# Cross attention and an ELU block on one core: state times w_in made per batch, one score matrix, 32x32 turns on VectorE

## The chip, the cores and the metric

The kernel runs on one core of a Trainium2 chip. The metric is the device time of one execution in microseconds (us), lower is better. In the views of the profile PE is TensorE's matmul, PEld its weight load, DVE VectorE, ACT ScalarE, POOL GpSimd and SP SyncE; L12 is line 12 of the kernel's file.

## What is computed

Eight batches of eight heads each have 512 tokens `x` and 32 rows of `state`, 64 wide. Tokens read the state and the state reads the tokens, from the same scores; both results go through a block of two matrices with ELU between them. `w_in` and `w_out` come as float64.

```python
B, H, S, Ns, D = (8, 8, 512, 32, 64)
scores = scale * np.matmul(x, state.transpose(0, 1, 3, 2))
scores = scores - scores.max(-1, keepdims=True)
a = np.exp(scores)
a /= a.sum(-1, keepdims=True) + 1e-09
xread = np.matmul(a, state)
scores2 = scale * np.matmul(state, x.transpose(0, 1, 3, 2))
...
a2 /= a2.sum(-1, keepdims=True) + 1e-09
sread = np.matmul(a2, x)
attn = np.concatenate([xread, sread], axis=2)      # (B, H, S + Ns, D)
x = attn.transpose(0, 2, 1, 3).reshape(B * (S + Ns), H * D)   # 4352 rows of 512
h = x @ w_in                                       # w_in 512 x 2048
g = np.where(h > 0.0, h, np.exp(np.minimum(h, 0.0)) - 1.0)
return g @ w_out                                   # w_out 2048 x 512
```

## The kernel before

Everything is float32; TensorE runs a float32 product as two instructions. One product of up to 512 columns fills one bank of PSUM. `ps_a` (three banks) serves attention, `ps_h` (three) the first matrix, `ps_o` (two) the second.

Setup loads the tokens of two batches and all states, turns the states (`k_bd`: 128 rows are two heads by 64, 128 columns are four heads by 32 state rows) and begins with the weights. `load_weights` fetches 512 float64 columns per partition and turns them into float32 on VectorE with seven operations; there are 16 such blocks of `w_in` and 16 of `w_out`. A block of `w_in` is 128 of the 2048 columns, all that one `ffn1` needs.

Attention of a batch is a list of 17 or 18 steps. `turn_x` turns the tokens of a pair of heads on TensorE (tile `xT`). `token_softmax` (`ts_ps`) takes tokens as rows and makes the softmax over the 32 state rows: maximum, subtraction and product on VectorE, exponential on ScalarE. `turn_token` (`tT_ps`) turns the weights back on TensorE, and `token_read` (`tr_ps`) multiplies them by the states, which gives `x2T`, the 512 model columns of what the tokens read, turned. `state_softmax` (`ss_ps`) makes the same scores once more, with state rows in the partitions, for the softmax over the tokens; its output has two halves of 64 partitions, each of one product with 64 columns of weights. `turn_state` (`sT_ps`) and `state_read` (`sr_ps`) use it.

The main loop goes over batches. `ffn1` runs 16 times for a batch: four products over the 512 model columns into `h_ps`, then ELU by a minimum on VectorE (PSUM to SBUF), an exponential on ScalarE and one last operation on VectorE. After each `ffn1` one step of the next batch's attention is emitted. Then `ffn2` runs for four groups of 128 tokens with 16 products each (`o_ps`). In batch 0 a block of `w_out` is loaded behind each `ffn1`. After the last batch, the 256 rows that the states read go through the same two matrices. A scheduler of the framework orders each engine's instructions from this program; on its engine an instruction then waits for its turn.

Of the kernel before, what the change touches and what calls it, by code (L numbers as in the profile page):

```python
# [19 lines left out]
def kernel(  # L20
# [7 lines left out]
):  # L28
    nc = tc.nc
# [17 lines left out]
    # The weights come as float64, here as the integers of the same bits.  # L47
# [5 lines left out]
    apool = ctx.enter_context(tc.tile_pool(name="attn", bufs=1))  # L53
# [3 lines left out]
    tpool = ctx.enter_context(tc.tile_pool(name="tok", bufs=2))  # L57
# [24 lines left out]
    x_t, st = {}, {}  # L82
# [9 lines left out]
    def setup():  # L92
        nc.vector.memset(v_bd, 0.0)
        make_identity(nc, ident)
        load_x(0)
# [6 lines left out]
        load_x(1)  # L102
# [15 lines left out]
        # The power of two, as the bits of a float32 with src's sign.  # L118
# [17 lines left out]
        # The mantissa, 1 to 2 times 2 ** 20: the high word's part is exact, the sum rounds.  # L136
# [18 lines left out]
    def turn_x(b, n):  # L155
        """x of a pair of heads, turned: rows (head, d), columns (r, p)."""
        ps = bank([P, R, P], "xT_ps")
        for r in range(R):
            nc.tensor.transpose(ps[:, r], x_t[b][:, r, n * P : (n + 1) * P], ident)  # L159
        nc.scalar.copy(out=st[b]["xT"][:, n], in_=ps)  # L160

    def state_softmax(b, g):
        """Rows (head of four, state row), over all tokens."""
        ps = bank([P, R, P], "ss_ps")
        for i in range(2):
# [3 lines left out]
                st[b]["xT"][:, 2 * g + i],  # L169
# [5 lines left out]
        nc.vector.reduce_max(top, ps.rearrange("p r q -> p (r q)"), axis=AX_X)  # L175
# [12 lines left out]

    def turn_state(b, g):
        ps = bank([P, R, P], "sT_ps")  # L190
        for r in range(R):
            nc.tensor.transpose(ps[:, r], st[b]["a_s"][:, g, r], ident)  # L192
        nc.scalar.copy(out=st[b]["aT_s"][:, g], in_=ps)

    def state_read(b):
        """Each pair's product of both heads with both: the two that belong are kept."""
        ps = bank([P, NP, 2 * NS], "sr_ps")
        for n in range(NP):
            i = n % 2
# [8 lines left out]
        for c in range(2):  # L208
            rows = slice(c * D, (c + 1) * D)
            nc.vector.tensor_copy(  # L210
                out=xT_state[rows, :, b * NS : (b + 1) * NS],
# [3 lines left out]
    def token_softmax(b, u):  # L215
        """Rows p, columns (r, head, state row), over the state rows; half of the r."""
        RH = R // 2
        ps = bank([P, RH, H * NS], "ts_ps")
        for i in range(RH):
            for n in range(NP):  # L220
                c = n % 2
                nc.tensor.matmul(  # L222
                    ps[:, i, n * D : (n + 1) * D],
                    st[b]["xT"][:, n, u * RH + i],
                    k_bd[:, b * G + n // 2, c * D : (c + 1) * D],
# [3 lines left out]
        top = small.tile([P, RH * H], FP32, name="top_t")  # L229
        total = small.tile([P, RH * H], FP32, name="total_t")  # L230
        a = st[b]["a_t"][:, u * RH : (u + 1) * RH].rearrange("p r (h n) -> p (r h) n", n=NS)
        s = ps.rearrange("p r (h n) -> p (r h) n", n=NS)
        nc.vector.reduce_max(top, s, axis=AX_X)
        nc.vector.tensor_tensor(out=a, in0=s, in1=bc(top, NS), op=ALU.subtract)
        nc.scalar.activation(out=a, in_=a, func=AF.Exp, scale=scale)
        nc.vector.reduce_sum(total, a, axis=AX_X)
        nc.vector.tensor_scalar(
            out=total, in0=total, scalar1=eps, scalar2=None, op0=ALU.add
        )
        nc.vector.reciprocal(out=total, in_=total)  # L240
        nc.vector.tensor_tensor(out=a, in0=a, in1=bc(total, NS), op=ALU.mult)

    def turn_token(b, g):
        ps = bank([P, R, P], "tT_ps")
        for r in range(R):
            nc.tensor.transpose(ps[:, r], st[b]["a_t"][:, r, g * P : (g + 1) * P], ident)  # L246
        nc.scalar.copy(out=st[b]["aT_t"][:, g], in_=ps)  # L247

    def token_read(b, n):
        rows = slice((n % 2) * D, (n % 2 + 1) * D)  # L250
        ps = bank([P, R, P], "tr_ps")
        nc.tensor.matmul(  # L252
            ps, v_bd[rows, b * G + n // 2], st[b]["aT_t"][rows, n // 2], start=True, stop=True
        )
        (nc.scalar.copy, nc.vector.tensor_copy)[n % 2](out=st[b]["x2T"][:, n], in_=ps)

    def begin(b):
        st[b] = dict(
            xT=apool.tile([P, NP, R, P], FP32, name="xT"),
            a_s=apool.tile([P, G, R, P], FP32, name="a_s"),  # L260
            aT_s=apool.tile([P, G, R, P], FP32, name="aT_s"),
            a_t=apool.tile([P, R, H * NS], FP32, name="a_t"),
            aT_t=apool.tile([P, G, R, P], FP32, name="aT_t"),
            x2T=tpool.tile([P, NP, R, P], FP32, name="x2T"),
        )
        turn_x(b, 0)
# [117 lines left out]
```

## Time and profile before

| | |
|---|---|
| time, median of 3 runs (lowest to highest) | 1136.9 us (1135.33 to 1138.26) |
| profiled execution: span from first to last instruction | 1135.5 us |
| TensorE busy (matmul) | 1086.1 us, 96% |
| VectorE busy | 384.5 us, 34% |
| ScalarE busy | 161.0 us, 14% |
| GpSimd busy | 18.0 us, 2% |
| HBM traffic over the span | 30 GB/s |

The page of the profile gives the span of the profiled execution and no other time of it; the span is 1.4 us below the median of the timed runs. A busy time is the union of an engine's instructions. Matmuls are pipelined, so a group's mean duration of one (593 to 599 ns for 512 columns) is longer than the distance from one to the next.

### The profile page before, as it was taken

The page shows a single profiled execution, that of the slowest core. Times are in us where ns is not written, and L with a number is a line of the kernel's source. Part 1 is how long each engine was busy: PE and PEld are TensorE (multiplying, and loading weights), DVE is VectorE, ACT ScalarE, POOL GpSimd, SP SyncE. Part 2 cuts the span into 40 slices and gives each one's busy share as a digit, 9 for nine tenths or more (in the row PEclk, how much of TensorE's full clock was granted, in tenths as well). Part 3 has the DMA queues.
Part 4 walks back from the last instruction along what each step waited for, and adds up shares of the span by engine and source line. Part 5 has one row for each costly group of instructions (what it writes and reads, how often), then busy time and mean ns, then how long its engine had stood idle before and what let it go on. Part 6 is the DMA issues. An engine that isn't in the chain of part 4 may idle for free.

```text
span 1135.5 us, 7859 instructions
## 1 busy us (share of the span) xinstructions
PE 1086.1 (96%) x3152; PEld 524.4 (46%) x3152; DVE 384.5 (34%) x742; ACT 161.0 (14%) x290; POOL 18.0 (2%) x26
## 2 busy tenths in 40 slices
PE   0679999999999999999999999999999999999998
PEld 0443454534445454534444454534444454444483
DVE  4989980441015300441015300441015300340040
ACT  0211310221012200221012200221012200110020
POOL 2000000000000000000000000000000000000000
PEclk8689999999999999999999999999999999999999
DMA  8363230000200010000200010000000000000000
GB/s 186 92 169 127 93 93 19 19 0 1 56 19 1 0 38 19 19 1 1 55 19 1 0 38 18 19 1 0 19 19 0 1 1 18 19 0 7 30 1 18
DMA packets 31588, 35.10 MB, mean 31 GB/s; under 512 B 17856, under 2 KB 26048, under 8 KB 31552
## 3 DMA queue, kind: packets, MB, share of 16 engines
q1 hardware_dynamic: 30080, 29.89, 8.6%
q0 software_dynamic: 1472, 4.72, 1.9%
q8 instruction: 24, 0.39, 0.1%
q14 instruction: 12, 0.10, 0.0%
HBM read 25.69 MB, written 8.91 MB: 30 GB/s over the span
## 4 chain that ended last, share of the span: by engine, by line
PE 94%; DVE 4%; DMA 1%; issue 0%; SPq 0%; ACT 0%
PE h_ps L286 41%; PE o_ps L305 41%; PE tr_ps L252 3%; PE sr_ps L201 3%; PE ts_ps L222 2%; PE xT_ps L159 1%; PE ss_ps L166 1%; DMA raw<-in_moe_w_in_dram 1%; DVE power L132 1%; PE sT_ps L192 1%; DVE w_in L141 1%; PE tT_ps L246 1%; DVE raw L137 0%; DVE power L128 0%; DVE power L124 0%; DVE power L119 0%
## 5 line engine op out<-in xcount | busy, mean ns | idle before, releaser
L286 PE MATMUL h_ps<-x2T,w_in 128*128 128x512 f32 x1024 | 465.3, 599 | 9.0 <-DVE g_sb L298 9.0
L305 PE MATMUL o_ps<-w_out,g_sb 128*128 128x512 f32 x1088 | 471.4, 593 | 0.0
L305 PEld LDWEIGHTS o_ps<-w_out,g_sb 128*128 128x128 f32 x1088 | 205.3, 190 | 252.3 <-issue 250.3
L286 PEld LDWEIGHTS h_ps<-x2T,w_in 128*128 128x128 f32 x1024 | 187.2, 191 | 238.1 <-issue 195.2
L295 DVE TENSOR_SCALAR e_sb<-h_ps 128x512 f32<-128x512 f32 (+1 forms) x144 | 95.1, 661 | 177.7 <-PE h_ps L286 177.5
L312 DVE COPY o_sb<-o_ps 128x512 f32<-128x512 f32 x17 | 11.8, 691 | 350.2 <-PE o_ps L305 350.2
L296 ACT ACTIVATE e_sb<-e_sb 128x512 f32<-128x512 f32 (+1 forms) x144 | 87.4, 607 | 279.6 <-DVE e_sb L295 257.9
L298 DVE SCALAR_TENSOR_TENSOR g_sb<-e_sb,h_ps 128x512 f32<-128x512 f32 (+1 forms) x144 | 93.9, 652 | 72.8 <-ACT e_sb L296 72.6
L312 ACT COPY o_sb<-o_ps 128x512 f32<-128x512 f32 x17 | 10.0, 587 | 335.4 <-PE o_ps L305 335.4
L160 ACT COPY xT<-xT_ps 128x512 f32<-128x512 f32 x32 | 18.5, 587 | 200.7 <-PE xT_ps L159 200.7
L210 DVE COPY xT_state<-sr_ps 64x128 f32<-64x128 f32 x16 | 4.6, 288 | 96.7 <-PE sr_ps L201 96.6
L252 PE MATMUL tr_ps<-aT_t,v_bd 64*128 64x512 f32 x64 | 34.8, 700 | 0.2 <-ACT aT_t L247 0.2
L106 PE MATMUL k_ps<-ident,v_bd 128*128 128x128 f32 x16 | 3.9, 426 | 31.9 <-DVE k_bd L107 18.1
L222 PEld LDWEIGHTS ts_ps<-k_bd,xT 128*128 128x128 f32 x256 | 30.7, 192 | 5.7 <-issue 5.7
L201 PEld LDWEIGHTS sr_ps<-aT_s,x_sb 128*128 128x128 f32 x256 | 30.7, 195 | 4.9 <-issue 4.3
L222 PE MATMUL ts_ps<-k_bd,xT 128*128 128x64 f32 x256 | 30.2, 272 | 0.0
L201 PE MATMUL sr_ps<-aT_s,x_sb 128*128 128x64 f32 x256 | 30.1, 276 | 0.0
L286 PE MATMUL h_ps<-xT_state,w_in 128*128 128x256 f32 x128 | 27.8, 379 | 0.0
L286 PEld LDWEIGHTS h_ps<-xT_state,w_in 128*128 128x128 f32 x128 | 24.3, 190 | 3.7 <-issue 0.5
L88 POOL DMA_DIRECT2D x_sb<-in_x_dram x16 | 14.8, 930 | 652.1 <-PE sr_ps L201 651.8
L159 PEld LDWEIGHTS xT_ps<-ident,x_sb 128*128 128x128 f32 x128 | 16.7, 148 | 14.5 <-issue 14.2
L132 DVE SCALAR_TENSOR_TENSOR power<-raw,power 128x512 uint32<-128x512 uint32 x32 | 21.8, 682 | 0.1
(45 smaller groups left out, 335.8 us busy)
## 6 DMA issues: line engine op xcount, KB each, us to landing
raw<-in_moe_w_in_dram SPq DMA_DIRECT2D x16, 512.0 KB, 3.7
raw<-in_moe_w_out_dram SPq DMA_DIRECT2D x16, 512.0 KB, 3.2
out_dram<-o_sb SPq DMA_DIRECT2D x16, 512.0 KB, 2.6
x_sb<-in_x_dram SPq DMA_DIRECT2D x16, 256.0 KB, 4.0
x_sb<-in_x_dram POOLq DMA_DIRECT2D x16, 256.0 KB, 5.5
v_bd<-in_state_dram POOLq DMA_DIRECT2D x4, 128.0 KB, 7.4
out_dram<-o_sb SPq DMA_DIRECT2D x8, 64.0 KB, 1.7
```

The lines of the kernel that those rows point to most:

```text
L132: nc.vector.scalar_tensor_tensor(out=power, in0=hi, scalar=0x80000000, in1=power, op0=ALU.bitwise_and, op1=ALU.bitwise_or,)
L159: nc.tensor.transpose(ps[:, r], x_t[b][:, r, n * P : (n + 1) * P], ident)
L160: nc.scalar.copy(out=st[b]["xT"][:, n], in_=ps)
L201: nc.tensor.matmul(ps[:, n], x_t[b][:, r, n * P : (n + 1) * P], st[b]["aT_s"][:, n // 2, r, i * D : (i + 1) * D], start=(r == 0), stop=(r ...
L222: nc.tensor.matmul(ps[:, i, n * D : (n + 1) * D], st[b]["xT"][:, n, u * RH + i], k_bd[:, b * G + n // 2, c * D : (c + 1) * D], start=True, ...
L252: nc.tensor.matmul(ps, v_bd[rows, b * G + n // 2], st[b]["aT_t"][rows, n // 2], start=True, stop=True)
L286: nc.tensor.matmul(ps, w_in[:, co, fo * P : (fo + 1) * P], xT[:, co], start=(co == 0), stop=(co == NP - 1),)
L295: nc.vector.tensor_scalar(out=e, in0=ps, scalar1=0.0, scalar2=None, op0=ALU.min)
L296: nc.scalar.activation(out=e, in_=e, func=AF.Exp)
L298: nc.vector.scalar_tensor_tensor(out=g[fo], in0=e, scalar=-1.0, in1=ps, op0=ALU.add, op1=ALU.max)
L305: nc.tensor.matmul(ps, g[fo][:, c * P : (c + 1) * P], w_out[:, fo], start=(fo == 0), stop=(fo == FO - 1),)
L312: (nc.scalar.copy, nc.vector.tensor_copy)[c % 2](out=o_sb[:, c % 2], in_=ps)
```

## The change

The tokens' weights times state times `w_in` are grouped the other way round. `make_m` multiplies the states of a batch by 512 columns of `w_in` (tile `m_sb`: 256 rows of four heads by state row twice, 512 columns), four times per batch, and `ffn1` contracts over those 256 rows: two products instead of four. `token_read` and `x2T` go. The scores are made once, with state rows in the partitions (`scores`, tile `s_ps`). For the softmax over the state rows VectorE turns the scores in blocks of 32x32 (`t_sb`), takes maximum and sum, GpSimd subtracts and multiplies, ScalarE makes the exponential; `turn_tokens` turns the blocks back on VectorE (tile `aT`). ELU's exponential now reads PSUM on ScalarE, and the minimum (with 1) follows on VectorE in SBUF. A block of `w_in` is now 512 columns of 128 rows, and the first `make_m` is emitted behind all 16 blocks. Token order within a batch, loads and `ffn2` stay.

```diff
-    apool = ctx.enter_context(tc.tile_pool(name="attn", bufs=1))
+    apool = ctx.enter_context(tc.tile_pool(name="attn", bufs=2))
+    xtpool = ctx.enter_context(tc.tile_pool(name="xT", bufs=4))
+    atpool = ctx.enter_context(tc.tile_pool(name="aT", bufs=4))
+    mpool = ctx.enter_context(tc.tile_pool(name="m", bufs=2))
...
-    def load_w_in(fo):
-        load_weights(w_in[:, :, fo * P : (fo + 1) * P], w_in_v[:, :, fo * P : (fo + 1) * P])
+    def load_w_in(c, n):
+        cols = slice(c * 512, (c + 1) * 512)
+        load_weights(w_in[:, n : n + 1, cols], w_in_v[:, n : n + 1, cols])
...
+    def scores(b, g):
+        ps = bank([P, S], "s_ps")
         for i in range(2):
             nc.tensor.matmul(
                 ps[i * D : (i + 1) * D],
                 k_bd[:, b * G + g, i * D : (i + 1) * D],
-                st[b]["xT"][:, 2 * g + i],
+                st[b, g, i],
...
+        t = apool.tile([P, NB, NS], FP32, name="t_sb")
+        nc.vector.transpose(t.rearrange("p k n -> p (k n)"), ps)
...
+        nc.vector.reduce_max(top_t, t, axis=AX_X)
+        nc.gpsimd.tensor_tensor(out=t, in0=t, in1=bc(top_t, NS), op=ALU.subtract)
+        nc.scalar.activation(out=t, in_=t, func=AF.Exp, scale=scale)
...
+        nc.vector.reduce_sum(total_t, t, axis=AX_X)
...
+        nc.gpsimd.tensor_tensor(out=t, in0=t, in1=bc(total_t, NS), op=ALU.mult)
+        st[b, g, "t"] = t
+
+    def turn_tokens(b, g):
+        st[b, g, "aT"] = atpool.tile([P, S], FP32, name="aT")
+        nc.vector.transpose(st[b, g, "aT"], st[b, g, "t"].rearrange("p k n -> p (k n)"))
...
+    def make_m(b, c):
+        m_t[b, c] = mpool.tile([P, G, 512], FP32, name="m_sb")
+        for g in range(G):
+            ps = bank([P, 512], "m_ps")
+            for i in range(2):
                 nc.tensor.matmul(
+                    ps[i * D : (i + 1) * D],
+                    k_bd[:, b * G + g, i * D : (i + 1) * D],
+                    w_in[:, 2 * g + i, c * 512 : (c + 1) * 512],
                     start=True,
                     stop=True,
                 )
+            (nc.scalar.copy, nc.vector.tensor_copy)[g % 2](out=m_t[b, c][:, g], in_=ps)
...
     def attention(b):
+        for g in range(G):
+            steps += [lambda g=g, i=i: turn_x(b, g, i) for i in range(2)]
+            steps += [lambda g=g: scores(b, g)]
+        for g in range(G):
+            steps += [lambda g=g: turn_tokens(b, g)]
+            steps += [lambda g=g: turn_state(b, g)]
+            steps += [lambda g=g: state_read(b, g)]
...
+    def elu(ps, g, fo):
+        e = epool.tile([P, n], FP32, tag="e", name="e_sb")
+        nc.scalar.activation(out=e, in_=ps, func=AF.Exp)
+        nc.vector.tensor_scalar(out=e, in0=e, scalar1=1.0, scalar2=None, op0=ALU.min)
...
+    def ffn1(g, b, fo):
+        for k in range(G):
+            nc.tensor.matmul(
+                ps,
+                m_t[b, fo // 4][:, k, fo % 4 * P : (fo % 4 + 1) * P],
+                st[b, k, "aT"],
...
+    todo = [lambda c=c, n=n: load_w_in(c, n) for c in range(FC) for n in range(NP)]
+    for f in attention(0):
         f()
+        if todo:
+            todo.pop(0)()
+    for f in todo:
+        f()
+    make_m(0, 0)
...
         for fo in range(FO):
-            ffn1(g, xT, fo)
+            ffn1(g, b, fo)
+            if fo % 4 == 1 and fo // 4 + 1 < FC:
+                make_m(b, fo // 4 + 1)
...
+            if c == 2 and b + 1 < B:
+                make_m(b + 1, 0)
```

How the instructions stand now, at three places. The first is TensorE in the ffn1 stage of a middle batch, between the last token score or state score and the turn behind it (`x4` is a count of products). Before:

```order
L166 MATMUL ss_ps<-xT,k_bd 64x512 x2
L286 MATMUL h_ps<-x2T,w_in 128x512 x4
L166 MATMUL ss_ps<-xT,k_bd 64x512 x2
L286 MATMUL h_ps<-x2T,w_in 128x512 x4
L246 MATMUL tT_ps<-ident,a_t 128x128 x4
```

After, at the same place; `s_ps` are the scores, `m_ps` the states times `w_in`:

```order
L253 MATMUL m_ps<-w_in,k_bd 64x512 x4
L175 MATMUL s_ps<-xT,k_bd 64x512 x2
L290 MATMUL h_ps<-aT,m_sb 128x512 x4
L224 MATMUL sT_ps<-ident,a_s 128x128 x4
L290 MATMUL h_ps<-aT,m_sb 128x512 x2
L233 MATMUL sr_ps<-aT_s,x_sb 128x64 x8
L290 MATMUL h_ps<-aT,m_sb 128x512 x2
L253 MATMUL m_ps<-w_in,k_bd 64x512 x4
```

An `ffn1` is two products, a make_m of four stands in one piece, and the state read follows the scores after three `ffn1` and one turn.

The second is TensorE at the end of batch 0, whose `o_ps` products need the blocks of `w_out` as they are converted. Before, then after:

```order
L305 MATMUL o_ps<-w_out,g_sb 128x512 x4
L286 MATMUL h_ps<-x2T,w_in 128x512 x4
L201 MATMUL sr_ps<-aT_s,x_sb 128x64 x8
L305 MATMUL o_ps<-w_out,g_sb 128x512
L201 MATMUL sr_ps<-aT_s,x_sb 128x64 x8
L305 MATMUL o_ps<-w_out,g_sb 128x512 x47
L286 MATMUL h_ps<-x2T,w_in 128x512 x4
```

```order
L253 MATMUL m_ps<-w_in,k_bd 64x512
L166 MATMUL xT_ps<-ident,x_sb 128x128 x4
L175 MATMUL s_ps<-xT,k_bd 64x512
L315 MATMUL o_ps<-w_out,g_sb 128x512 x2
L290 MATMUL h_ps<-aT,m_sb 128x512
L175 MATMUL s_ps<-xT,k_bd 64x512
L315 MATMUL o_ps<-w_out,g_sb 128x512 x2
L290 MATMUL h_ps<-aT,m_sb 128x512
L315 MATMUL o_ps<-w_out,g_sb 128x512 x2
L290 MATMUL h_ps<-aT,m_sb 128x512 x3
L315 MATMUL o_ps<-w_out,g_sb 128x512 x34
L290 MATMUL h_ps<-aT,m_sb 128x512 x2
```

Ahead of the 34 `o_ps` products there now stand 38 `h_ps` products (32 of batch 0, 6 of batch 1), six make_m, 40 turns of `xT` and five `s_ps` steps from the program's start; before, only batch 0's `h_ps` stand ahead of the last 47.

The third is ScalarE at the first of these places: the exponential of the states' weights (`a_s`), that of the turned scores (`t_sb` now, `a_t` before), those of ELU (`e_sb`) and the copies of the turned weights (`aT_s`). Before:

```order
L235 ACTIVATE a_t<-a_t 128x512
L296 ACTIVATE e_sb<-e_sb 128x512
L180 ACTIVATE a_s,total<-ss_ps,top 128x512
L296 ACTIVATE e_sb<-e_sb 128x512
L180 ACTIVATE a_s,total<-ss_ps,top 128x512
```

After:

```order
L260 COPY m_sb<-m_ps 128x512
L192 ACTIVATE a_s,total<-s_ps,top 128x512
L279 ACTIVATE e_sb<-h_ps 128x512
L200 ACTIVATE t_sb<-t_sb 128x512
L279 ACTIVATE e_sb<-h_ps 128x512
L226 COPY aT_s<-sT_ps 128x512
L279 ACTIVATE e_sb<-h_ps 128x512 x2
```

The exponential of the turned scores, whose input comes from GpSimd, stands one ELU exponential behind that of the states, with the next ELU exponential and the copy for the state read queued behind it.

## Rows read from the trace of the kernel before

**Rows 1.** The page: span, and busy time of the engines.

```profile
span 1135.5 us, 7859 instructions
...
PE 1086.1 (96%) x3152; PEld 524.4 (46%) x3152; DVE 384.5 (34%) x742; ACT 161.0 (14%) x290; POOL 18.0 (2%) x26
```

**Rows 2.** Windows: stretch, length, each engine's busy us, granted clock, DMA share, GB/s.

```profile
40.00:60.00 20.00, 16.89 (x77) 10.90 (x76) 15.34 (x38) 6.14 (x12) 0.00 (x0) 0.74 0.26 77
60.00:80.00 20.00, 17.04 (x85) 10.68 (x84) 18.68 (x42) 2.88 (x5) 1.87 (x2) 0.97 0.64 170
80.00:165.30 85.30, 78.56 (x216) 35.99 (x217) 85.20 (x184) 15.51 (x27) 2.21 (x2) 0.95 0.36 114
198.20:326.14 127.94, 127.94 (x370) 59.99 (x369) 33.55 (x60) 18.89 (x34) 1.76 (x2) 1.00 0.06 17
```

**Rows 3.** The chain that ended last: start us, us, what; batch 0's end, last batch, tail.

```profile
157.81 40.40 PE o_ps L305 x94
...
965.84 54.93 PE h_ps L286 x128
1020.78 54.93 PE o_ps L305 x128
1075.71 27.63 PE h_ps L286 x128
1103.34 27.48 PE o_ps L305 x64
```

**Rows 4.** The same chain within one middle batch, one row of each kind.

```profile
198.20 3.43 PE h_ps L286 x8
201.64 0.44 PE xT_ps L159 x4
...
217.13 1.73 PE ts_ps L222 x16
218.86 3.49 PE h_ps L286 x8
...
227.57 1.01 PE ss_ps L166 x4
228.58 3.63 PE h_ps L286 x8
...
244.59 1.05 PE tr_ps L252 x2
...
281.37 3.52 PE sr_ps L201 x32
```

**Rows 5.** The timeline of VectorE: first conversion, one inside a block, the last.

```profile
16.81 0.43 DVE L119 TENSOR_SCALAR power<-raw 128x512 uint32<-128x512 uint32 x1 [13.81 <-DMA raw<-in_moe_w_in_dram]
...
21.36 0.68 DVE L132 SCALAR_TENSOR_TENSOR power<-raw,power 128x512 uint32<-128x512 uint32 x1
21.96 0.42 DVE L119 TENSOR_SCALAR power<-raw 128x512 uint32<-128x512 uint32 x1
22.29 0.42 DVE L137 TENSOR_SCALAR raw<-raw 128x512 uint32<-128x512 uint32 x1
...
164.65 0.69 DVE L144 SCALAR_TENSOR_TENSOR w_out<-w_out,power 128x512 f32<-128x512 f32 x1
```

**Rows 6.** Groups by line and shape: count, busy us, mean ns, idle before.

```profile
L295 DVE TENSOR_SCALAR e_sb<-h_ps 128x512 f32<-128x512 f32 x128 | 88.4, 690 | 171.6 <-PE h_ps L286 171.4
...
L166 PE MATMUL ss_ps<-xT,k_bd 128*64 128x512 f32 x64 | 17.3, 617 | 0.5 <-DVE a_t L234 0.5
...
L234 DVE TENSOR_TENSOR a_t<-ts_ps,top_t 128x512 f32<-128x512 f32 x16 | 10.9, 685 | 0.2
```

**Rows 7.** The timeline while GpSimd issues two transfers in the front.

```profile
61.50 1.87 POOL L88 DMA_DIRECT2D x_sb<-in_x_dram  x2 [53.61 <-PE sr_ps L201]
...
62.81 0.79 DVE L137 TENSOR_SCALAR raw<-raw 128x512 uint32<-128x512 uint32 x1
```

**Rows 8.** Groups by line: the one elementwise operation of GpSimd.

```profile
masks.py:199 POOL TENSOR_SCALAR_AFFINE_SELECT ident<-ident 128x128 f32<-128x128 f32 x1 | 0.3, 306 | 0.1
```

More of the change, by code (lines that the diff above doesn't have):

```diff
@@ L38 @@
     FO = DF // P
+    FC = DF // 512
     SB = S + NS
+    NB = S // 32
     scale = 1.0 / math.sqrt(D)
@@ L101, in setup @@
             )
-        load_x(1)
+        for b in range(2):
+            load_x(b)
         for k in range(0, B * G, 4):
@@ L210, in state_read @@
             nc.vector.tensor_copy(
-                out=xT_state[rows, :, b * NS : (b + 1) * NS],
+                out=xT_state[rows, 2 * g : 2 * g + 2, b * NS : (b + 1) * NS],
                 in_=ps[rows, :, c * NS : (c + 1) * NS],
             )
[L215 to L221, printed above, removed]
+    def make_m(b, c):
+        m_t[b, c] = mpool.tile([P, G, 512], FP32, name="m_sb")
+        for g in range(G):
+            ps = bank([P, 512], "m_ps")
+            for i in range(2):
                 nc.tensor.matmul(
-                    ps[:, i, n * D : (n + 1) * D],
-                    st[b]["xT"][:, n, u * RH + i],
-                    k_bd[:, b * G + n // 2, c * D : (c + 1) * D],
+                    ps[i * D : (i + 1) * D],
+                    k_bd[:, b * G + g, i * D : (i + 1) * D],
+                    w_in[:, 2 * g + i, c * 512 : (c + 1) * 512],
                     start=True,
@@ L228, in token_softmax @@
                 )
[L229 to L266, printed above, removed]
-    def attention(b):
-        steps = [lambda: begin(b)]
-        steps += [lambda n=n: turn_x(b, n) for n in range(1, NP)]
-        steps += [lambda u=u: token_softmax(b, u) for u in range(2)]
-        steps += [lambda g=g: state_softmax(b, g) for g in range(G)]
-        steps += [lambda g=g: turn_token(b, g) for g in range(G)]
-        steps += [lambda n=n: token_read(b, n) for n in range(NP)]
-        steps += [lambda g=g: turn_state(b, g) for g in range(G)]
-        steps += [lambda: state_read(b)]
+            (nc.scalar.copy, nc.vector.tensor_copy)[g % 2](out=m_t[b, c][:, g], in_=ps)
@@ L277, in attention @@
+    def attention(b):
+        steps = []
+        for g in range(G):
[5 more added lines that the diff above has]
+            steps += [lambda g=g: state_read(b, g)]
         if b + 2 < B:
@@ L279, in attention, with ffn1_state @@
         return steps
-    def ffn1(g, xT, fo):
-        n = xT.shape[-1]
-        ps = ps_h.tile([P, n], FP32, tag="h", name="h_ps")
+    def elu(ps, g, fo):
+        n = ps.shape[-1]
+        e = epool.tile([P, n], FP32, tag="e", name="e_sb")
+        nc.scalar.activation(out=e, in_=ps, func=AF.Exp)
+        nc.vector.tensor_scalar(out=e, in0=e, scalar1=1.0, scalar2=None, op0=ALU.min)
+        g[fo] = gpool.tile([P, n], FP32, tag="g", name="g_sb")
+        nc.vector.scalar_tensor_tensor(
+            out=g[fo], in0=e, scalar=-1.0, in1=ps, op0=ALU.add, op1=ALU.max
+        )
+    def ffn1(g, b, fo):
+        ps = ps_h.tile([P, S], FP32, tag="h", name="h_ps")
+        for k in range(G):
[3 more added lines that the diff above has]
+                st[b, k, "aT"],
+                start=(k == 0),
+                stop=(k == G - 1),
+            )
+        elu(ps, g, fo)
+    def ffn1_state(g, fo):
+        ps = ps_h.tile([P, B * NS], FP32, tag="h", name="h_ps")
         for co in range(NP):
@@ L288, in ffn1 @@
                 w_in[:, co, fo * P : (fo + 1) * P],
-                xT[:, co],
+                xT_state[:, co],
                 start=(co == 0),
@@ L314 @@
     setup()
-    for i, f in enumerate(attention(0)):
-        f()
-        if i >= 4 and i % 4 == 0:
-            load_w_in(i // 4 - 1)
-    begun = i // 4
-    for fo in range(begun, FO):
-        load_w_in(fo)
+    todo = [lambda c=c, n=n: load_w_in(c, n) for c in range(FC) for n in range(NP)]
+    for f in attention(0):
+        f()
+        if todo:
[3 more added lines that the diff above has]
+    make_m(0, 0)
     for b in range(B):
@@ L345 @@
     for fo in range(FO):
-        ffn1(g, xT_state, fo)
+        ffn1_state(g, fo)
     o_sb = opool.tile([P, 2, DM], FP32, name="o_sb")
```

51 lines of the change are left out of this document (24 added, 27 removed).

## The prediction

> **What bounds the kernel now.** I read the busy shares first: TensorE is busy for 1086.1 of the 1135.5 us [rows 1]. The page gives the span alone as the profiled execution's time; the median of the timed runs is 1136.9 us, 1.4 more, and I add that 1.4 at the end. A busy share is a mean over stages, so I next read windows by stage [rows 2]: from 198.20 to 326.14 us, one middle batch, TensorE is busy all the time and VectorE for 33.55 of 127.94 us; from 80 to 165.30 us VectorE is busy for 85.20 of 85.30 us. So there are two stages, a front that VectorE fills with the conversion of the weights, and a long rest that TensorE fills. The chain of work shows the same [rows 3]: from 157.81 us on, nothing but TensorE pieces follow each other to 1130.82 us. What the change is worth is thus TensorE's saving in the rest, plus whatever happens to the moment at which the front lets go.
>
> **One middle batch on TensorE, before.** The chain inside it [rows 4] prices every step. Eight h instructions (four float32 products, two instructions each) take 3.43 us, 0.429 each. A turn of four 128x128 blocks takes 0.44. A ts step takes 1.73, and the h block behind it 3.49 instead of 3.43: 1.79 together. An ss step takes 1.01, and the h block behind it 3.63: 1.21 together. A tr step takes 1.05 plus the same 0.20: 1.25. The state read takes 3.52. There are eight turns (4 xT, 2 tT, 2 sT: 3.52), two ts (3.58), two ss (2.42), four tr (5.00), one state read (3.52), 128 h and 128 o instructions (54.93 each, as in the last batch [rows 3]): 127.90, where the rows show 326.14 - 198.20 = 127.94.
>
> **The same batch after.** ffn1 contracts over 256 columns of M instead of 512 of the model: 64 h instructions fewer, -27.47. The ts steps go (-3.58), the two tT turns (-0.88), the four tr steps (-5.00). The s steps are the old ss steps. New are four make_m per batch, of 4 products or 8 instructions each, with k_bd as 64-column weights and 512 columns streamed. No row shows it; the nearest is ss, the same shape [rows 4, 6]: four instructions of 617 ns mean fit into 1.01 us, so the two halves of the output run side by side, two by two (2 x 0.43), and 1.21 - 0.86 = 0.35 is the price of going into that form and back. make_m streams two such groups in one go: 2 x 0.86 + 0.35 = 2.07. Bounds: 1.72 if nothing is paid for the change of form, 2.42 if each group pays. I take 2.07, since both groups stand together in the order. Four: +8.28. The batch comes to 127.94 - 27.47 - 3.58 - 0.88 - 5.00 + 8.28 = 99.3. The last batch has no attention behind it and three make_m: 54.93 + 27.46 + 6.2 = 88.6. The tail (27.63 + 27.48) stays.
>
> **The front.** VectorE's first conversion starts at 16.81 us and its last ends at 165.3 [rows 5], 148.5 us, of which 6.0 idle (4.66 and 1.32 [rows 2]): 142.5 of work. The 32 conversions stay. By the order of the changed program, up to its last conversion: 16 minima of ELU now read SBUF, not PSUM; 690 ns [rows 6] against 0.42 us for the like form over SBUF [rows 5], -4.3. Operations of 0.68 follow each other at 0.60, those of 0.42 at 0.33 [rows 5]. Four copies of x2T go: -2.4. Six copies of M come ahead of that row: +3.6. Four more small xT_state copies: +1.0. One reduction of the next batch: +0.6. Eight elementwise operations (685 ns [rows 6]) go to GpSimd and eight 32x32 turns come: no row shows such a turn; between 0.42 (the fast form) and twice 685 ns this is -2 to +5, and I take 0, one element a cycle like the rest. Sum: 141.0, no relief for the front. To it come the old 6.0 idle and new waiting. GpSimd's eight elementwise operations of batches 0 and 1 lie in this stretch. Their price: one operation on 128x128 took 306 ns [rows 8], four times that is 1.22 for 128x512; bounds 0.69 (VectorE's own) and 2.45 (two inputs, one after the other); I take 1.4. When GpSimd works, VectorE's operations beside it can stretch: 0.79 us instead of 0.42 while GpSimd issued two transfers [rows 7]. If each GpSimd operation held VectorE throughout, that is 8 x 1.4 = 11 us. Besides, M of the first columns is emitted behind all w_in conversions, so the first h can start only behind 61 us of VectorE's work and some 9 of waits, at about 87 us, and TensorE has 79 us of ordered work (38 h, 30 o, six make_m and the rest) between there and the end of the front: both engines are nearly full, and a delay of one is passed on, up to 5 us. New waiting 0 to 16, taken as 8. The front ends at 16.8 + 141.0 + 6 + 8 = 172 us instead of 165.
>
> The Trainium skill ("SBUF — State Buffer", Who interferes with whom) says that GpSimd and a VectorE operation in a 2-port mode, or with two SBUF inputs, fully block each other for the whole instruction. By it the 11 us are paid in full and the front ends near 175; the stretched row agrees in kind, as an estimate only, since that GpSimd work was descriptors.
>
> **What remains behind the front.** In the order, 34 o products stand behind the last conversion (29.2 us: rows 3's 40.40 for 94 instructions, 68 here). Batch 1 has by then 6 h products, one make_m, two turns and one s step done: 99.3 - 5.15 - 2.07 - 0.88 - 1.21 = 90.0. Then five batches (496.5), the last (88.6), the tail (55.1): 759.4 us. The last copy and transfer take 1135.5 - 1130.8 = 4.7 as before.
>
> **Waits inside a batch.** ffn1 has half the work, so VectorE and ScalarE have less cover. VectorE: 16 x (0.34 + 0.60) for ELU, two score steps of 3.8, four copies and small ones, some 26 us in an ffn1 stage of 42 us; no bound. But ScalarE's queue is in order, and the exponential of the turned scores stands there ahead of the exponential of an h block and of the copy of aT_s, which the state read needs. From the end of an s step: maximum 0.60, scaling 0.08, turn 0.60, maximum 0.60, GpSimd 1.4, exponential 0.63 and about 1.0 of handovers make 4.9; then exponential 0.63 and copy 0.59: 6.1. TensorE meanwhile does three h blocks and one turn, 3 x 1.72 + 0.44 = 5.6. So 0.5 to 1 us is missing once a batch, and each us that GpSimd takes longer is one more. Bounds 0 (GpSimd 0.69) to 4 us a batch; I take 1.4: 10 us for seven batches.
>
> The Trainium skill ("GPSIMD Engine Reference", 3.1 Elementwise) measures tensor_tensor at 1.96 times VectorE's time; against 0.60 this is an estimate of 1.2 us, and the sum would be some 3 us less. No row here shows such an operation.
>
> **Sum.** 172 + 759.4 + 10 + 4.7 = 946 us of span, 947 as a time: 190 us less, 17%.
>
> **Rivals.**
> *GpSimd blocks and is blocked all the way.* If its operations take about 4 us each, because VectorE holds it off again and again, then each of the 14 groups delays both the exponential and the turn behind the second operation by 2.6 us. TensorE has one to two h blocks in hand (three PSUM buffers), so about 3 of 5.2 us come through: 14 x 3 = 42 more in place of 10, and the front 11 rather than 8: 982. For it: rows 7, and that VectorE is full in the front. Against: in a middle batch VectorE has 26 us of work in 42 us of ffn1, so GpSimd finds it idle often.
> *The two halves of make_m do not run side by side.* Then 8 x 0.43 + 0.35 = 3.79 instead of 2.07, for 26 make_m behind the front +45: 992. Against it is the ss row.
> *Slower than before.* It takes one thing: GpSimd's elementwise operation at 10 us or more. There are 28 in the loop, each in series with ScalarE's and VectorE's queues, and 190 us over 28 is 6.8 beyond the 1.4 assumed and about 2 of slack. At 12 us: 946 + 28 x (12 - 3.4) = 1187. Against it speaks 306 ns for 128x128.
> *The front hides the gain.* If VectorE stayed the bound beyond batch 0, the saving would shrink. It doesn't: behind the last conversion it has 27 us of work in 99.
>
> **How the numbers follow.** Forecast (TensorE stays the bound, waits up to 3 us a batch): 0.70, and its own range is 918 to 972. GpSimd rival: 0.18. Halves in turn: 0.05. Slower: 0.02. Better than all terms (no idle in the front, 158; make_m at 1.72; no waits): 158 + 750 + 4.7 + 1.4 = 914, and beyond: 0.05. The range 915 to 990 takes in the forecast, the front's bounds and most of the GpSimd rival. A measurement of this kernel tells about 0.3% from no change: faster 0.97, within 0.01, slower 0.02.
>
> **What will show it.** Right: middle batches of 99 to 101 us with TensorE full; make_m at about 2.07; the last w_out conversion near 172 us; GpSimd's operations between 1.2 and 2 us. Wrong: TensorE idle ahead of sr or h with ScalarE or VectorE as the releaser (GpSimd rival); make_m near 3.8; VectorE's conversions stretched beside GpSimd all through the front, or a front past 185 us; a turn on VectorE above 0.7 us.

## The result, and the profile after

The changed kernel takes 932.4 us (median of four runs, 930.75 to 932.92) where the kernel before takes 1136.6 us on the same chip (1135.33 to 1138.26): 0.820 of it, 95% interval 0.8188 to 0.8211. The forecast was 947 us, 1.6% too high. The page of the changed kernel's profile, span and busy times, against [rows 1]:

```profile
span 931.1 us, 6560 instructions
...
PE 872.7 (94%) x2512; PEld 401.3 (43%) x2512; DVE 363.1 (39%) x774; ACT 156.9 (17%) x290; POOL 53.1 (6%) x58
```

TensorE lost 213.4 us of busy time and the span 204.4 us, so nearly all of it came through. The windows by stage are cut at the same stages as [rows 2]; the first row here is the whole stretch of the weights' conversion.

```profile
16.80:165.37 148.57, 108.83 (x323) 48.47 (x323) 142.38 (x316) 26.11 (x48) 13.53 (x12) 0.87 0.41 121
...
40.00:60.00 20.00, 16.04 (x56) 10.51 (x56) 17.14 (x42) 3.70 (x7) 7.11 (x6) 0.58 0.43 105
60.00:80.00 20.00, 7.10 (x20) 1.74 (x19) 18.36 (x41) 1.76 (x3) 0.00 (x0) 0.67 0.52 160
80.00:165.37 85.37, 78.65 (x221) 32.20 (x221) 84.99 (x188) 17.72 (x32) 6.42 (x6) 0.96 0.36 111
286.58:386.16 99.58, 99.58 (x290) 44.51 (x290) 30.45 (x64) 18.42 (x34) 6.04 (x6) 1.00 0.08 22
```

The two stages are still there. From 80 us to the last conversion VectorE is busy for 84.99 of 85.37 us; in a middle batch TensorE is busy without a gap. New is the row from 60 to 80 us, in which TensorE works for 7.1 us where it worked for 17.0 before: M of the first columns has to wait for all of `w_in`. The end of the front is still 165.37 us (165.3 before); what that wait costs, the run m_early below tells. The chain of work that ended last, against [rows 3]:

```profile
165.53 2.58 PE h_ps L290 x6
168.11 29.27 PE o_ps L315 x68
...
230.01 41.20 PE o_ps L315 x96
...
329.16 41.20 PE o_ps L315 x96
...
816.43 54.93 PE o_ps L315 x128
871.37 27.63 PE h_ps L303 x128
898.99 27.48 PE o_ps L315 x64
```

A middle batch is 329.16 - 230.01 = 99.15 us (127.94 before, 99.3 forecast). The same chain inside one middle batch, against [rows 4]:

```profile
290.88 1.87 PE m_ps L253 x8
292.75 0.59 PE xT_ps L166 x4
...
302.29 1.87 PE m_ps L253 x8
304.16 0.86 PE s_ps L175 x4
305.01 3.63 PE h_ps L290 x8
308.64 0.44 PE sT_ps L224 x4
309.08 1.72 PE h_ps L290 x4
310.80 0.00 issue
310.80 2.00 PE sr_ps L233 x16
...
314.57 1.87 PE m_ps L253 x8
316.44 1.91 PE h_ps L290 x4
...
320.51 1.73 PE sr_ps L233 x16
```

A make_m is 1.87 us and lengthens what stands behind it by 0.15 (an `xT` turn, 0.59 for 0.44) or 0.19 (h, 1.91 for 1.72): 2.02 to 2.06, where 2.07 was forecast. Where a score step stands directly behind it (304.16), the form of the product does not change and 0.35 us is saved. Of waiting there is 0.27 us. It lies inside the state read, whose weight load starts only with it (310.80 us), behind the copy of `aT_s`: the first state read takes 2.00 us where the second has 1.73. Groups by line and shape (busy us, mean ns of one, idle before), against [rows 6]:

```profile
L279 ACT ACTIVATE e_sb<-h_ps 128x512 f32<-128x512 f32 x128 | 76.2, 595 | 300.4 <-PE h_ps L290 295.9 <-DVE raw L144 4.0
L253 PE MATMUL m_ps<-w_in,k_bd 128*64 128x512 f32 x256 | 68.1, 622 | 1.5 <-ACT xT L168 0.8 <-ACT m_sb L260 0.7
L280 DVE TENSOR_SCALAR e_sb<-e_sb 128x512 f32<-128x512 f32 x128 | 54.3, 424 | 82.3 <-ACT e_sb L279 82.3
...
L199 POOL TENSOR_TENSOR t_sb<-t_sb,top_t 128x512 f32<-128x512 f32 x16 | 17.8, 1115 | 570.0 <-DVE top_t L198 445.4 <-DVE total L202 122.3 <-DVE total_t L209 2.3
L213 POOL TENSOR_TENSOR t_sb<-t_sb,total_t 128x512 f32<-128x512 f32 x16 | 17.5, 1092 | 38.9 <-DVE total_t L212 38.9
L218 DVE STREAM_TRANSPOSE aT<-t_sb 128x512 f32<-128x512 f32 x16 | 11.3, 708 | 8.5 <-POOL t_sb L213 8.5
...
L206 DVE TENSOR_SCALAR a_s<-a_s,total 128x512 f32<-128x512 f32 x16 | 10.7, 666 | 0.2
```

GpSimd's operations take 1.1 us (forecast 1.4, with 1.2 to 2 named as the sign of being right), the 32x32 turn 0.71, the minimum 0.42 where it took 0.69 from PSUM.

### The profile page after: what moved, and what is told of

Its sections match the earlier page's. It is cut to its first block, busy times and chain, and to the rows that moved or that the text cites. A ratio compares the mean times of both kernels' runs of the same rounds, so it can differ in the third digit from the quotient of the medians.

```text
span 931.1 us, 6560 instructions
## 1 busy us (share of the span) xinstructions
PE 872.7 (94%) x2512; PEld 401.3 (43%) x2512; DVE 363.1 (39%) x774; ACT 156.9 (17%) x290; POOL 53.1 (6%) x58
## 4 chain that ended last, share of the span: by engine, by line
PE 88%; DVE 8%; DMA 3%; SPq 1%; ACT 0%; issue 0%; POOL 0%; DVEq 0%; ACTq 0%
PE o_ps L315 49%; PE h_ps L290 23%; PE m_ps L253 6%; PE h_ps L303 3%; DMA raw<-in_moe_w_in_dram 3%; PE sr_ps L233 3%; PE s_ps L175 2%; PE xT_ps L166 2%; DVE power L139 1%; DVE w_in L148 1%; DVE power L126 1%; DVE raw L144 1%; PE sT_ps L224 1%; DVE power L131 1%; DVE power L135 1%; DVE w_in L151 0%
## 5 line engine op out<-in xcount | busy, mean ns | idle before, releaser
L290 PE MATMUL h_ps<-aT,m_sb 128*128 128x512 f32 x512 | 242.1, 606 | 12.8 <-DVE m_sb L260 12.6
L290 PEld LDWEIGHTS h_ps<-aT,m_sb 128*128 128x128 f32 x512 | 92.3, 193 | 123.1 <-issue 82.7
L279 ACT ACTIVATE e_sb<-h_ps 128x512 f32<-128x512 f32 (+1 forms) x144 | 82.4, 572 | 335.4 <-PE h_ps L290 295.9
L280 DVE TENSOR_SCALAR e_sb<-e_sb 128x512 f32<-128x512 f32 (+1 forms) x144 | 59.0, 410 | 98.4 <-ACT e_sb L279 98.4
L253 PE MATMUL m_ps<-w_in,k_bd 128*64 128x512 f32 x256 | 68.1, 622 | 1.5 <-ACT xT L168 0.8
L260 DVE COPY m_sb<-m_ps 128x512 f32<-128x512 f32 x32 | 22.0, 688 | 91.0 <-PE m_ps L253 89.5
L199 POOL TENSOR_TENSOR t_sb<-t_sb,top_t 128x512 f32<-128x512 f32 x16 | 17.8, 1115 | 570.0 <-DVE top_t L198 445.4
L233 PEld LDWEIGHTS sr_ps<-aT_s,x_sb 128*128 128x128 f32 x256 | 33.9, 209 | 10.9 <-ACT aT_s L226 6.4
L253 PEld LDWEIGHTS m_ps<-w_in,k_bd 128*64 128x64 f32 x256 | 15.8, 138 | 46.5 <-issue 35.3
L233 PE MATMUL sr_ps<-aT_s,x_sb 128*128 128x64 f32 x256 | 34.5, 292 | 1.4 <-ACT aT_s L226 1.3
L166 PE MATMUL xT_ps<-ident,x_sb 128*128 128x128 f32 x128 | 21.4, 295 | 3.1 <-DVE xT_state L242 3.0
L260 ACT COPY m_sb<-m_ps 128x512 f32<-128x512 f32 x32 | 18.8, 586 | 22.9 <-PE m_ps L253 22.9
```

The costliest lines, as they stand in the source:

```text
L166: nc.tensor.transpose(ps[:, r], x_t[b][:, r, (2 * g + i) * P : (2 * g + i + 1) * P], ident)
L233: nc.tensor.matmul(ps[:, i], x_t[b][:, r, (2 * g + i) * P : (2 * g + i + 1) * P], st[b, g, "aT_s"][:, r, i * D : (i + 1) * D], start=(r == 0),
L253: nc.tensor.matmul(ps[i * D : (i + 1) * D], k_bd[:, b * G + g, i * D : (i + 1) * D], w_in[:, 2 * g + i, c * 512 : (c + 1) * 512], start=Tr ...
L260: (nc.scalar.copy, nc.vector.tensor_copy)[g % 2](out=m_t[b, c][:, g], in_=ps)
L279: nc.scalar.activation(out=e, in_=ps, func=AF.Exp)
L280: nc.vector.tensor_scalar(out=e, in0=e, scalar1=1.0, scalar2=None, op0=ALU.min)
```

## The experiments

Ratios are to the kernel before, with 95% intervals. "The front's end" is the end of the last conversion of `w_out`; "o" is the start of the first long row of o products in the chain (168.11 us in the changed kernel).

### GpSimd's operations doubled (pool_twice)

```diff
+        nc.gpsimd.tensor_tensor(out=t, in0=t, in1=bc(top_t, NS), op=ALU.subtract)
...
+        nc.gpsimd.tensor_tensor(out=t, in0=t, in1=bc(ones, NS), op=ALU.mult)
```

> The changed kernel with each of GpSimd's elementwise operations followed by a second one of the same size (the maximum is subtracted twice, which the softmax cancels, and the product is multiplied by one). Theory (no slack is left between the exponential of the turned scores and the state read): 1.1 us more come through once a batch, 7 to 8 us, and 2 to 4 in the front: 939 to 945 us. Rival A (GpSimd is hidden): 932 to 935 us. Rival B (GpSimd stands in series everywhere): 28 x 1.1 and the front, 963 us or more.

967.6 us, 0.852 (0.850 to 0.8535): 35 us more than the changed kernel, and my theory fell. The time lies in the range of rival B; whether each operation costs alike, as rival B has it, the next two runs tell. 7.5 us of it are in the front (o at 175.64 us) and 5.5 in each of four middle batches ((760.51 - 341.88) / 4 = 104.66 us); the batch shown here, the one ahead of them, takes 103.78 (238.10 to 341.88), 4.6 more. The timeline of this kernel in a middle batch shows the way; L201 and L202 are the two subtractions, L216 and L217 the two products, `aT` the first group's turn, `top` the second group's maximum:

```profile
312.07 1.03 PE L177 MATMUL s_ps<-xT,k_bd 128*64 128x512 f32 x4
...
313.50 1.05 POOL L217 TENSOR_TENSOR t_sb<-t_sb,ones 128x512 f32<-128x512 f32 x1
314.58 0.71 DVE L222 STREAM_TRANSPOSE aT<-t_sb 128x512 f32<-128x512 f32 x1 [1.69 <-POOL t_sb L217]
...
315.22 0.65 DVE L264 COPY m_sb<-m_ps 128x512 f32<-128x512 f32 x1
315.79 0.67 DVE L186 TENSOR_REDUCE top<-s_ps 128x1 f32<-128x512 f32 x1
...
319.12 1.05 POOL L202 TENSOR_TENSOR t_sb<-t_sb,top_t 128x512 f32<-128x512 f32 x1
...
319.16 1.29 DVE L209 TENSOR_SCALAR a_s<-a_s,total 128x512 f32<-128x512 f32 x1
320.20 0.63 ACT L203 ACTIVATE t_sb<-t_sb 128x512 f32<-128x512 f32 x1 [2.27 <-POOL t_sb L202]
320.74 0.58 ACT L283 ACTIVATE e_sb<-h_ps 128x512 f32<-128x512 f32 x1
321.21 0.58 ACT L230 COPY aT_s<-sT_ps 128x512 f32<-128x512 f32 x1
...
321.84 0.32 PE L237 MATMUL sr_ps<-aT_s,x_sb 128*128 128x64 f32 x1 [2.95 <-ACT aT_s L230]
```

The second group's scores end at 313.0 us, but VectorE stands in front of the first group's turn, which waits 1.69 us for GpSimd, and a copy is queued behind it too; the maximum starts at 315.8, 2.8 us after the scores instead of 0.9 in the changed kernel. Then the doubled subtraction holds ScalarE's queue, in which the copy of `aT_s` stands behind the exponential of the turned scores. Both together are the 2.95 us for which TensorE waits. The rest of the 4.6 us comes behind the wait: the state read takes 2.42 us instead of 1.73 and the h block behind it 3.03 instead of 1.77, at a granted clock of 0.72 between 323 and 329 us. The changed kernel has next to no slack here: its copy of `aT_s` ends 5.73 us after the scores, and TensorE has 5.79 us of other work.

### Which of the two operations (sub_twice, mul_twice)

Each doubles one of the two lines of the diff above.

> GpSimd's subtraction is doubled, its product not (a second subtraction of the same maximum, so the weights' values change; the amount of work does not). Theory: what counts is the way from the second group's scores to aT_s, which ScalarE's queue makes pass through the subtraction but not through the product. In a middle batch the doubled subtraction then adds its own 1.1 us and some 0.45 us by which the first group's turn holds VectorE when the second group's maximum is due: 1.6 us of waiting at the state read, and 0 to 2 us of slower TensorE behind it, 2 to 3.5 us a batch; with some 4 us at the front: 945 to 956 us, and each middle batch shows one wait of 1.3 to 2 us ahead of sr_ps with aT_s as the releaser. Rival (every us on GpSimd costs alike, by the shared port or by any of its two consumers): half of what both doublings cost, 949 us here and 949 us for the doubled product.

> GpSimd's product is doubled (the second time by ones), its subtraction not. Theory: the product is not on the way to aT_s; it counts only through the first group's turn, behind which the second group's maximum waits on VectorE: 0.45 us a batch at most, and up to 4 us at the front: 933 to 939 us, no wait of more than 1.2 us ahead of sr_ps in a middle batch. Rival (every us on GpSimd costs alike): 949 us.

958.8 us, 0.8434 (0.8418 to 0.845), for the subtraction; 941.2 us, 0.8281 (0.8265 to 0.8298), for the product. They cost 26.5 and 8.8 us, not the same, so the rival is out; but both lie some 2 to 3 us above the theory's ranges. The product costs 1.06 us in most middle batches (330.67 to 430.87: 100.20), one wait of 1.05 us ahead of the state read, more than twice the 0.45 that I gave: the first group's turn ends at 305.93 us, 0.5 after the scores, and two operations of ELU, the copy of `m_sb` and the maximum all stand behind it. The subtraction costs 4.1 us a batch ((752.33 - 339.28) / 4 = 103.26), more than its wait of 2.0 us. Windows of this kernel from the start of that wait on (columns as in rows 2) show the rest:

```profile
315.60:317.60 2.00, 0.00 (x0) 0.00 (x0) 1.97 (x4) 1.64 (x4) 0.32 (x1) 1.00 0.02 4
317.60:324.69 7.09, 7.09 (x22) 4.66 (x24) 3.17 (x9) 0.45 (x1) 1.05 (x1) 0.52 0.00 1
324.69:332.36 7.67, 7.67 (x38) 4.33 (x38) 3.35 (x6) 2.86 (x5) 0.00 (x0) 1.00 0.00 0
```

After 2 us in which TensorE did nothing, its granted clock is 0.52 for the next 7.09 us, close to the lower of its two levels (1.2 of 2.4 GHz), and then 1.00 again: the state read takes 3.68 instead of 1.73 us, the h block behind it 3.41 instead of 1.77, 3.6 us for a wait of 2. The five middle batches take 102.83 to 104.50 us (this one is 104.50), and what comes behind the wait is 1.9 to 3.6 us; why they differ was not tried. Behind the wait of 1.05 us of mul_twice the clock stays at 1.00 in four of the five middle batches. In the other one (531.08 to 632.92: 101.84 us) the h block behind the state read takes 3.07 us instead of 1.77 and the make_m behind that 2.21 instead of 1.87, 1.6 us for a wait of 1.05; the window of that h block:

```profile
614.92:617.99 3.07, 3.07 (x6) 0.81 (x7) 1.99 (x5) 0.00 (x0) 1.17 (x2) 0.55 0.00 0
```

### GpSimd's two operations on VectorE (vector_elem)

```diff
-        nc.gpsimd.tensor_tensor(out=t, in0=t, in1=bc(top_t, NS), op=ALU.subtract)
+        nc.vector.tensor_tensor(out=t, in0=t, in1=bc(top_t, NS), op=ALU.subtract)
```

and the product likewise.

> The changed kernel with the two elementwise operations of the turned scores on VectorE instead of GpSimd. Theory: eight of them lie in the front, 8 x 0.60 = 4.8 us, less some 1 to 2 us by which GpSimd stretched VectorE there; middle batches stay at 99 us, since VectorE has room: 932 to 937 us. Rival (the move to GpSimd is worth something in every batch): 4 x 0.6 a batch come through, 948 us or more.

931.0 us, 0.8195 (0.8183 to 0.8208): no different from the changed kernel's 932.4, 1 us below the theory's range, and the rival is out. So this part of the change is worth nothing. In a middle batch the 0.27 us of waiting is gone (o at 229.43 and 328.32: 98.89); each operation takes 0.68 us there instead of 1.05 and more, and needs no handover to another engine. In the front, eight more operations of VectorE did not make it end later: 165.09 against 165.37 us. Part of the reason is in the groups of VectorE over the conversions: beside GpSimd, the first bit operation of a conversion (L126) takes 469 ns in the mean, the last of a `w_in` block (L151) 713, and ELU's minimum 451; here 429, 682 and 418. Times their 31, 16 and 16 that is 1.2 + 0.5 + 0.5 = 2.3 us, by which VectorE is slower beside GpSimd, while GpSimd saves it eight operations at 0.60, 4.8 us. The difference, 2.5 us, and the 0.3 by which the front even ended sooner, stay open; the records of a few of VectorE's operations are missing in either trace, so its busy times over the front are not exact enough for that.

### ELU as before (elu_old)

```diff
-        nc.scalar.activation(out=e, in_=ps, func=AF.Exp)
-        nc.vector.tensor_scalar(out=e, in0=e, scalar1=1.0, scalar2=None, op0=ALU.min)
+        nc.vector.tensor_scalar(out=e, in0=ps, scalar1=0.0, scalar2=None, op0=ALU.min)
+        nc.scalar.activation(out=e, in_=e, func=AF.Exp)
```

> The changed kernel with ELU in its old order (minimum from PSUM on VectorE, then the exponential on ScalarE). Theory (VectorE sets the front, TensorE the rest): 16 minima of batch 0 cost 0.27 us more each, so the front ends 4.3 us later, the middle batches stay at 99.2 us: 936 to 937 us. Rival (the new order is what keeps ffn1 fed now that it is half as long): TensorE waits in ffn1, batches of 101 to 104 us, 945 to 965 us.

933.4 us, 0.8216 (0.8204 to 0.8228), about 1 us more than with the new ELU, with overlapping intervals: less than the theory's, and the rival is out. The relief of the front is real: it ends at 169.13 us, 3.76 later than in the changed kernel (4.3 forecast). But o starts at 169.52, only 1.4 later, for in the changed kernel TensorE still has 2.58 us of h to do when the front lets go, and here TensorE has all but 0.4 us of that behind it when the last conversion ends. In each middle batch 0.17 us come back (330.40 - 231.42 = 98.98), with a first state read of 1.82 us instead of 2.00.

### M as one chain of two products (m_serial)

```diff
                 nc.tensor.matmul(
-                    ps[i * D : (i + 1) * D],
-                    k_bd[:, b * G + g, i * D : (i + 1) * D],
+                    ps,
+                    k_bd[:, b * G + g],
                     w_in[:, 2 * g + i, c * 512 : (c + 1) * 512],
-                    start=True,
-                    stop=True,
+                    start=(i == 0),
+                    stop=(i == 1),
```

M becomes a sum of two products here, so the output is another; the instructions and their sizes along the tokens stay.

> make_m with both products 128 weight columns wide into the whole bank, the second added to the first, so that they cannot run side by side (M is then a sum of two products, not the right M). Theory: a make_m takes 8 x 0.43 = 3.43 us instead of 2.07 and pays no change of form: +1.36 for each of the 26 behind the front: 967 us, up to 8 more if the six in the front come through. Rival (the halves did not overlap before either, and make_m is cheap for another reason): 930 to 936 us.

966.9 us, 0.8503 (0.8489 to 0.8517), as expected. The chain inside a middle batch of this kernel:

```profile
305.91 3.43 PE m_ps L253 x8
309.34 1.01 PE s_ps L175 x4
...
319.64 3.43 PE m_ps L253 x8
323.07 1.72 PE h_ps L290 x4
```

Eight instructions take 3.43 us instead of 1.87, and nothing behind them is lengthened. A batch takes 335.60 - 230.84 = 104.76 us, 5.6 more. Eight instructions in 1.87 us are less than eight times 0.43, so in the changed kernel they do overlap. The pairing of the two halves is worth 34.5 us, and the rival of the forecast in which they do not run side by side is out.

### The regrouping alone (regroup_only)

The kernel before with `make_m`, two products per `ffn1` and no `token_read`; its own two score matrices, turns on TensorE and ELU stay.

```diff
-        for co in range(NP):
+        for k in range(G):
             nc.tensor.matmul(
                 ps,
-                w_in[:, co, fo * P : (fo + 1) * P],
-                xT[:, co],
+                m_t[b, fo // 4][:, k, fo % 4 * P : (fo % 4 + 1) * P],
+                st[b]["aT_t"][:, k].rearrange("p r q -> p (r q)"),
```

> The kernel before with one part of the change alone: make_m and an ffn1 of two products, w_in in blocks of 512 columns; the tokens' softmax is still made on its own scores and turned on TensorE. Theory: a middle batch is 127.94 - 27.47 - 5.00 + 8.28 = 103.8 us and the last 88.6, the front within 5 us of the changed kernel's: 958 us, 952 to 966. Rival (the single score matrix is worth as much as the regrouping): 1000 us or more.

965.5 us, 0.8493 (0.848 to 0.8505), at the upper end. A middle batch takes 344.53 - 240.89 = 103.64 us (127.94 before): the regrouping is 171 of the 204 us, and the rest of the change (one score matrix, turns on VectorE, the new ELU) the other 33. Of these, 4.5 in each of five middle batches are TensorE's ts steps and turns, 3.6 more lie between the o of batch 0 and that of batch 1 (65.48 us for 61.90), and 7.3 are the later start of o (175.41 against 168.11), for the front ends only at 174.40 us.

### The first M earlier (m_early)

```diff
     for f in attention(0):
         f()
         if todo:
             todo.pop(0)()
+        if len(todo) == 12:
+            make_m(0, 0)
     for f in todo:
         f()
-    make_m(0, 0)
```

> The changed kernel with the first make_m emitted behind the first four blocks of w_in instead of behind all sixteen. Theory: TensorE begins ffn1 some 20 us earlier, but w_out is converted no sooner, so the last conversion stays at 165 us and the time moves by at most 3 us: 929 to 935. Rival (TensorE's wait of 12.6 us for the first copy of M is lost time): 920 us or less.

931.6 us, 0.8198 (0.8185 to 0.821): the same as the changed kernel. There TensorE waits 12.6 us for its first `m_sb`. Here M is ready early, and the same h waits 10.9 us for ELU instead, which VectorE does only between conversions. The front ends at 162.07 us, 3.3 sooner, and o starts at 166.26, 1.85 sooner, too little for the medians to tell. An idle TensorE cost 1.85 us at most there, because VectorE is what sets the front's end.

### A shorter conversion (conv_short, conv_early, conv_vector)

If VectorE sets the front, fewer operations on it must shorten the whole. Three operations, shown below, make a float32 out of the bits of a float64 instead of seven. They hold for weights of a magnitude below 2 and not below 2^-126, and cut the last bits off instead of rounding. conv_early adds the edit of m_early, conv_vector that of vector_elem to both.

```diff
+        nc.vector.tensor_scalar(
+            out=power, in0=hi, scalar1=3, scalar2=0x3FFFFFF8,
+            op0=ALU.logical_shift_left, op1=ALU.bitwise_and,
+        )
+        nc.vector.scalar_tensor_tensor(
+            out=power, in0=hi, scalar=0x80000000, in1=power,
+            op0=ALU.bitwise_and, op1=ALU.bitwise_or,
+        )
+        nc.vector.scalar_tensor_tensor(
+            out=dst.bitcast(U32), in0=lo, scalar=29, in1=power,
+            op0=ALU.logical_shift_right, op1=ALU.bitwise_or,
+        )
```

> The changed kernel with three VectorE operations for a block of weights instead of seven (exponent and mantissa bits shifted together; the low bits are cut off instead of rounded, and it holds for magnitudes below 2 only). Theory: 32 x (3.15 - 1.54) = 51 us less on VectorE in the front; TensorE then has to do its 838 us from its first ffn1 at about 58 us on: 895 to 912 us. Rival (the transfer of 17 MB of weights sets the front): 920 us or more.

> Both: three operations for a block of weights, and the first make_m behind the first four blocks of w_in. Theory: with VectorE no longer the bound of the front, TensorE's start counts: its first ffn1 some 10 us earlier than with the short conversion alone, 885 to 902 us. Rival (transfers or VectorE still set the front): the same time as with the short conversion alone.

> The shorter conversion and the early make_m as in conv_early, and the two elementwise operations on VectorE instead of GpSimd. Theory: with VectorE no longer full in the front, its eight more operations there cost nothing, and the wait ahead of the state read (0.27 us a middle batch) goes as it did in vector_elem: 896 to 898.5 us. Rival (the front of conv_early still hangs on VectorE at places, and eight operations of 0.6 us more are passed on): 900 to 905 us.

903.6, 899.5 and 898.8 us, ratios 0.7949 (0.7935 to 0.7962), 0.7913 (0.7902 to 0.7925) and 0.7907 (0.7893 to 0.7921). The front now ends at 118.9 us in conv_short and 115.3 in conv_early, 46 to 50 us sooner, and 29 to 33 come through. Windows of conv_short say why not all:

```profile
60.00:80.00 20.00, 20.00 (x63) 7.47 (x63) 15.62 (x35) 7.71 (x15) 1.05 (x1) 1.00 0.56 192
80.00:117.00 37.00, 37.00 (x119) 18.16 (x118) 36.81 (x76) 8.93 (x16) 5.86 (x5) 1.00 0.55 171
```

From 60 us on TensorE is busy all the time, though VectorE still converts until 118.9: the bound has passed to TensorE 58.9 us before the conversions end, and I conclude, without a run that shows it, that a conversion saved after that would shorten nothing. An M made earlier is worth 4 us there (conv_early), where it was worth nothing while VectorE was full. The first two lie in their theories' ranges; conv_vector is 0.3 us above its own and below its rival's. conv_vector and conv_early are not told apart: the batch gains 0.27 us (295.91 - 197.02 = 98.89), and the long o row from which that is counted begins 1.4 us later (197.02 against 195.58).

## Why the prediction was right, and where its sizes were off

**Bound and saving.** The forecast that TensorE stays the bound behind the front and VectorE in it holds in every window above. The middle batch came out at 99.15 us for 99.3 without waits and 100.7 with them. Against the 99.3 the differences are small and in part cancel, which is luck: make_m 2.02 to 2.06 for 2.07, one change of form fewer (-0.35), a wait of 0.27. m_serial shows that the two halves do run side by side.

**The front.** This is the first mis-sized term: "new waiting", taken as 8 us, measured as 2.5. 172 us were forecast for its end and 165.37 measured. VectorE's work was put at 141.0 us without stretching and is 142.38 with it, about 2.3 of it by GpSimd. Idle were 6.2 us where 6 and "new waiting" of 8 were taken. So of the 8, waiting makes 0.2 and stretching 2.3 (0 to 11 was its bound). Four more products of GpSimd in the front (mul_twice) let it end only 0.45 us later, four more subtractions (sub_twice) 4.2. The coupling of TensorE's delay to VectorE, up to 5, is 3.3 at most by m_early. A late TensorE delayed VectorE by no more than that; conversions, which need nothing from TensorE, stand in VectorE's queue between what does.

The Trainium skill ("SBUF — State Buffer", Who interferes with whom) has VectorE and GpSimd block each other by a lock on a shared port pair. Rows here agree in kind: the two-input last operation of a conversion, 0.68 us alone, took 1.20 between 44.34 and 45.54 us beside a subtraction and a product of GpSimd:

```profile
43.48 1.50 POOL L199 TENSOR_TENSOR t_sb<-t_sb,top_t 128x512 f32<-128x512 f32 x1 [2.31 <-DVE total_t L209]
...
44.34 1.20 DVE L151 SCALAR_TENSOR_TENSOR w_in<-w_in,power 128x512 f32<-128x512 f32 x1
44.94 1.49 POOL L213 TENSOR_TENSOR t_sb<-t_sb,total_t 128x512 f32<-128x512 f32 x1
```

But by that rule I had given the front's end as near 175, and it is 165.37; GpSimd's own operation was stretched from 1.05 to 1.50 us, so part of the conflict was paid by GpSimd, and most of VectorE's operations in the front kept the time that they have in vector_elem.

**Behind the front.** 759.4 us were forecast from the last conversion on, and from o (168.11) to the chain's end (926.47) it is 758.4, with the waits inside. Between the front's end and o stand 2.7 us that the sum did not have: three of batch 1's first six h products, which it took as done by then. So the 15.0 us between the forecast span of 946.1 and the measured 931.1 are -6.6 at the front's end, +2.7 up to o, -11.0 behind it (769.4 with the waits against 758.4) and -0.1 at the end.

**Waits inside a batch.** The second mis-sized term: 10 us taken, 0.27 a middle batch measured. The chain from the scores to `aT_s` is 5.73 us (6.1 forecast), mainly because GpSimd takes 1.05 instead of 1.4, and TensorE's cover 5.79 (5.6 forecast). The sentence "each us that GpSimd takes longer is one more" has the right place but the wrong size: a microsecond costs 1.06 in most batches through the product, which the sum did not have on the way at all, and 4.1 through the subtraction, because a TensorE that waits 2 us then runs slower.

The Trainium skill's figure ("GPSIMD Engine Reference", 3.1 Elementwise), an estimate of 1.2 us, was nearer than my 1.4: 1.05 us beside nothing, 1.09 to 1.12 in the mean. Its ratio of 1.96 is not what the runs show: VectorE takes 0.68 us for the same operation (vector_elem), so the ratio is 1.5 to 1.6, and the estimate came near because it set the ratio against 0.60, the step from one operation to the next.

**The 32x32 turn.** 0.60 us from one to the next was taken and a duration above 0.7 called wrong; it lasts 0.70 to 0.71 and the next starts 0.63 behind it. That is 0.03 for each of the eight in the front: nothing.

**The other rivals.** GpSimd's blocking all the way needed operations of 4 us; they take 1.1, and the longest in the front 1.50. The slower case needed 10. The front did not hide the gain.

## What to carry to other kernels

Regroup a product of three so that the long side of the work is contracted over the shorter one, and count what is added with the form in which it runs: two 64-column halves side by side cost half of one chain. Before work is moved to another engine, follow each of its results to what is queued behind the consumer in order; here an operation "off the path" stood ahead of the next group's maximum. Price a late operand by what it does after the wait too, and an earlier operand only by what the engine that sets the stage's end can make of it.

## What the hardware showed that was not expected

- A wait of 2.0 us on TensorE was followed by 7.09 us at a granted clock of 0.52, in which TensorE took 3.6 us longer for the same work, so it cost 5.6 us in all. A wait of 1.05 us cost only itself in four batches, and in a fifth 1.6 us more, with a granted clock of 0.55 behind it.
- GpSimd's subtraction and product on 128x512 float32 take 1.05 us undisturbed and up to 1.50 beside VectorE; the scaling of `a_s` on VectorE, 0.48 alone, took 0.87 to 1.30 beside them.
- A 32x32 turn of 128x512 float32 on VectorE, from PSUM or SBUF, costs 0.70 to 0.71 us, about the 0.67 to 0.69 us of a maximum, a sum or an operation on two inputs of that size there.
